# Attention and a cosine-gated FFN on one core: attention matmuls merged into bursts of fixed order, the weight conversion redistributed, softmax sums moved to PSUM

## The chip, the cores and the metric

The kernel runs on one core of a Trainium2 chip. The metric is device time in microseconds (us). Three timed executions gave 1001.33, 1002.23 and 1008.99 us (median 1002.23); a further one was taken by the hardware profiler.

## The reference, cut to what matters

Eight batches, eight heads, 576 positions, head size 64. The first four heads see the last 32 positions, the other four see every 32nd position; softmax, then the FFN with `h * cos(h)`. All in float32.

```python
scores = scale * np.matmul(q, k.transpose(0, 1, 3, 2))
scores = np.where(masks[None], scores, -1e9)
attn = np.exp(scores - np.max(scores, axis=-1, keepdims=True))
attn = attn / (np.sum(attn, axis=-1, keepdims=True) + 1e-09)
x = np.matmul(attn, v) ...          # (8*576, 512) after joining the heads
h = x @ w_in                        # 4608 x 2048
out = (h * np.cos(h)) @ w_out       # 4608 x 512
```

## The kernel before, in words

**FFN.** The 4608 tokens are cut in 12 blocks of 384 (index `j`), the 2048 hidden columns in 16 slices of 128 (index `f`). One pair (j, f) is a chunk. `hidden` makes 12 matmuls into one of two PSUM banks `h` (L345): the float32 operands are split in a high and a low fp32r part, and three products of the parts are summed for four slices of the depth. Then ScalarE rounds h/2pi to an integer (L349), VectorE takes the remainder (L350), ScalarE the sine (L353), VectorE multiplies by `h` (L356) and thereby frees the bank, ScalarE cuts the high part `g_hi` (L359) and GpSimd the low part `g_lo` (L360). `outer` makes 9 matmuls into three accumulators (L367); it runs three chunks (`LAG`) behind `hidden`.

**Attention.** 80 units, ten for each batch: four strided ones (heads with every 32nd position) and six local ones. A unit is a generator of three steps: (1) its score matmuls into a PSUM bank (L238 local, L279 strided) and its softmax; (2) transposes of the probabilities (L246 local, L291 strided) and a copy to SBUF; (3) the products with v (L254 local, L303 strided) and a copy, and a DMA to the tensor `xT` in DRAM, from which `load_x` reads the FFN's blocks. The softmax of the main part is a chain of eleven instructions: mask added (L193, VectorE), maximum (L194, VectorE), subtraction (L195, GpSimd), two Silu (L203, L204, ScalarE), their combination (L205, VectorE), square (L208, ScalarE), sum (L210), 1e-9 added (L211), reciprocal (L212, all VectorE), scaling (L214, GpSimd).

**Stages.** First the 20 units of batches 0 and 1 alone (`plain`: the mask is put in by a matmul, exp is used, and small `keep_busy` matmuls fill TensorE, L417). Then the blocks j = 0 and 1, chunk by chunk in turn, while the weights are brought in: `load_weight` takes 128x512 float64 values as two int32 words and puts them together as float32 (L116, L119 and L125 on VectorE, L124 on ScalarE), cuts the high part (L129, ScalarE) and the low part (L130, GpSimd); 32 of these, in two buffers (`cv`), two for each f. `need_weights` places those of f so that VectorE starts them no earlier than the remainder of chunk (0, f-2). Then the main part: blocks 2 to 11, 160 chunks, the first three still within the loading part; the 60 units of batches 2 to 7 run beside them. Here the score bank is one tile, cleared once (L181) and kept; the transposes have another bank and the products a third.

**Order.** `schedule` gives each unit three places among the chunks: its start from the line through `KNOTS` ((chunk, unit number) pairs), step 2 up to three chunks later, step 3 one chunk after that. This sets the order in which the program names the instructions; the framework that places them may move an instruction of TensorE ahead of others that it expects to wait. Every engine then runs its own list in order, with semaphores between the engines.

Of the kernel before, what the change touches and what calls it, by code (L numbers as in the profile page):

```python
# [12 lines left out]
F32 = mybir.dt.float32  # L13
F32R = mybir.dt.float32r
BF16 = mybir.dt.bfloat16
I32 = mybir.dt.int32
AF = mybir.ActivationFunctionType
ALU = mybir.AluOpType
AX = mybir.AxisListType

B, H, S, D = 8, 8, 576, 64
# [3 lines left out]
P = 128  # L25
# [31 lines left out]

KNOTS = ((LAG, 0), (9.5, 8), (25, 16), (121, 56), (131, 60))
UNIT_LAG = 3
LOAD_AT = 13  # L60
# [8 lines left out]
def attention_cos_ffn(ctx, tc, qkl, vl, qkvs, w_in, w_out, eye, eye16, mask_l0, mask_l, mask_s, out):  # L69
# [41 lines left out]
    def load_weight(cv, src, hi, lo, after):  # L111

        raw = cv.tile([P, 512, 2], I32, name="raw")
        nc.sync.dma_start(out=raw.rearrange("p n w -> p (n w)"), in_=src)
        low, top = raw[:, :, 0], raw[:, :, 1]
        first = nc.vector.tensor_scalar(out=low, in0=low, scalar1=29, scalar2=None, op0=ALU.logical_shift_right)  # L116
        if after is not None:
            order(first, after, "weights no earlier than they are needed")
        nc.vector.scalar_tensor_tensor(  # L119
            out=low, in0=top, scalar=-0x80000000, in1=low, op0=ALU.bitwise_and, op1=ALU.bitwise_or  # L120
        )


        nc.scalar.activation(out=top.bitcast(F32), in_=top.bitcast(F32), func=AF.Copy, scale=2.0 ** -112)  # L124
        nc.vector.scalar_tensor_tensor(  # L125
            out=low, in0=top, scalar=3, in1=low, op0=ALU.logical_shift_left, op1=ALU.bitwise_or
        )
        w = low.bitcast(F32)
        nc.scalar.copy(out=hi, in_=w)  # L129
        nc.gpsimd.tensor_tensor(out=lo, in0=w, in1=hi.bitcast(F32), op=ALU.subtract)  # L130

    weights = 0

    def need_weights(cv, f):
        nonlocal weights
        for f in range(weights, f + 1):
# [6 lines left out]
            weights = f + 1  # L143

    class Attention:

        def __init__(self, stack, plain, scores, transposed, products, ld_bufs):

            self.plain = plain
            self.ld, self.wk = (
                stack.enter_context(tc.tile_pool(name=name, bufs=bufs, side="right", reuse_waits="tile"))
                for name, bufs in (("ld", ld_bufs), ("wk", 2))
            )
            self.scores, self.transposed, self.products = (
                itertools.cycle(kind) for kind in (scores, transposed, products)
            )
            self.turns, self.kept = itertools.cycle(range(len(scores))), {}
            self.pn_s = itertools.cycle(pn_s)  # L160
            self.x_t = {}

        def bank(self, kind):
# [19 lines left out]

        def softmax(self, s, mask, n, w, pn=None):
            t = self.wk.tile([P, SU * GB], F32, name="t_sb")[:, :n * w].rearrange("p (t w) -> p t w", w=w)
# [23 lines left out]
            z = sm.tile([P, SU], F32, name="z")  # L209
            nc.vector.tensor_reduce(out=z[:, :n], in_=e, op=ALU.add, axis=AX.X)  # L210
            nc.vector.tensor_scalar(out=z[:, :n], in0=z[:, :n], scalar1=1e-9, scalar2=None, op0=ALU.add)  # L211
            nc.vector.reciprocal(out=z[:, :n], in_=z[:, :n])  # L212
            pn = e if pn is None else pn
# [11 lines left out]
        def local(self, b, p, u):  # L225
# [8 lines left out]
            for t in range(LU):  # L234
                for j in range(2):
                    rows = slice(64 * j, 64 * j + 64)
                    lo = STRIDE if u + t == 0 else 0
                    self.scored = nc.tensor.matmul(  # L238
                        s_ps[rows, t * KW + lo:(t + 1) * KW], q_t[rows, QB * t:QB * (t + 1)],
                        k_t[rows, QB * t + lo:QB * t + KW], start=not self.plain, stop=True, skip_group_check=True,  # L240
                    )
            pn = self.softmax(s_ps[:, :LU * KW].rearrange("p (t w) -> p t w", w=KW), mask, LU, KW)
            yield
            t_ps = self.bank(self.transposed)
            for t in range(LU):
                nc.tensor.transpose(t_ps[:KW, t * P:(t + 1) * P], pn[:, t], ident)  # L246
            pt = self.wk.tile([P, LU * P], F32, name="pt")
# [4 lines left out]
            for t in range(LU):  # L252
                for j in range(2):
                    nc.tensor.matmul(  # L254
                        a_ps[64 * j:64 * j + 64, t * QB:(t + 1) * QB], v_t[:, t, j],
                        pt[:KW, t * P + 64 * j:t * P + 64 * j + QB], start=True, stop=True, skip_group_check=True,
                    )
            nc.scalar.copy(out=x_t, in_=a_ps[:, :LU * QB])
# [3 lines left out]
        def strided(self, b, p, u):  # L262
# [11 lines left out]
            for t in range(SU):  # L274
                for i in range(2):
                    if SU * u + t // 2 * 2 + i >= NG:
                        continue
                    rows = slice(64 * i, 64 * i + 64)
                    self.scored = nc.tensor.matmul(  # L279
                        s_ps[64 * i:64 * i + GB, t * GB:(t + 1) * GB], q_t[rows, t], k_t[rows, t],  # L280
                        start=not self.plain, stop=True, skip_group_check=True,
                    )
            pn = next(self.pn_s)
            self.softmax(
                s_ps[:, :SU * GB].rearrange("p (t w) -> p t w", w=GB), mask,
                SU, GB, pn[:, :, :GB],
            )
            yield
            t_ps = self.bank(self.transposed)
            for t in range(0, SU, 2):  # L290
                nc.tensor.transpose(t_ps[:, t * GP:(t + 2) * GP], pn[:, t:t + 2].rearrange("p t k -> p (t k)"), ident)  # L291
            pt = self.wk.tile([P, LU * P], F32, name="pt")
# [7 lines left out]
            for t in range(real):  # L300
                for j in range(2):
                    keys = slice(64 * j, 64 * j + GB)
                    nc.tensor.matmul(  # L303
                        a_ps[64 * j:64 * j + 64, t * GB:(t + 1) * GB], v_t[keys, t],
                        pt[keys, t * GB:(t + 1) * GB], start=True, stop=True, skip_group_check=True,
                    )
            x_v = x_t.rearrange("p (a r) -> p a r", r=STRIDE)
# [33 lines left out]
    def hidden(j, f, x_hi, x_lo):  # L341
        h = ps_h.tile([P, 512], F32, name="h")[:, :TB]
        ops = [(w, x, c) for c in range(NKC) for w, x in ((wi_h, x_hi), (wi_h, x_lo), (wi_l, x_hi))]
        for i, (w, x, c) in enumerate(ops):
            nc.tensor.matmul(h, w[:, f, c], x[c], start=(i == 0), stop=(i == len(ops) - 1))  # L345

# [16 lines left out]
    def outer(j, f, g_hi, g_lo, acc):  # L363
        for t in range(NTT):
            ts = slice(t * P, (t + 1) * P)
            for i, (g, w) in enumerate(((g_hi, wo_h), (g_hi, wo_l), (g_lo, wo_h))):
                nc.tensor.matmul(  # L367
                    acc[t], g[:, ts], w[:, f], start=(f == 0 and i == 0), stop=(f == NFC - 1 and i == 2)
                )
            if f == NFC - 1:  # L370
# [16 lines left out]

    def schedule(units, knots, lag):

# [3 lines left out]
        for n, (at, unit) in enumerate(zip(begun, units)):  # L393
            second = min([at + lag] + begun[n + 2:n + 3])
            for stage in (at, second, second + 1):
                steps.setdefault(stage, []).append((n, unit))
        return steps

    def step(steps, n):
        for _, unit in steps.get(n, ()):  # L400
            next(unit, None)

    with ExitStack() as loading:
        cv = loading.enter_context(tc.tile_pool(name="cv", bufs=2))
        with ExitStack() as stack:

            ps = stack.enter_context(tc.tile_pool(name="ps", bufs=1, space=bass.MemoryType.PSUM, reuse_waits="tile"))
            att = Attention(
                stack, True, ((ps_h, "h"), (ps_h, "h"), (ps, "acc0")), ((ps_o, "acc0"), (ps_o, "acc1")),
                ((ps_o, "acc2"), (ps, "acc3")), ld_bufs=3,  # L410
            )
            steps = schedule(att.units(0) + att.units(1), ((0, 0), (20, 20)), 2)
            spare = ps.tile([P, 512], F32, name="acc2")

            def keep_busy(n, after):
                for _ in range(n):
                    mm = nc.tensor.matmul(  # L417
                        spare[:64], warm, warm.unsqueeze(1).broadcast_to([P, 8, 64]), start=True, stop=True
                    )
# [146 lines left out]
```

## Time and profile before

| | |
|---|---|
| timed executions | 1001.33, 1002.23, 1008.99 us |
| the profiled execution | 1007.06 us, of which the span from first to last instruction is 1005.2 us |
| mean granted TensorE clock | 0.992 |
| busy: TensorE, VectorE, ScalarE, GpSimd | 983.1, 472.4, 502.9, 382.3 us |

A row of a group reads: line, engine, operation, written tile <- read tiles, shape, count | busy us, mean ns of one | idle time of the engine before them and what ended it. A row of the timeline reads: start in us, duration in us, engine, line, operation, count, and in brackets the idle time before it and what ended it. Matmuls are pipelined, so the distance from one start to the next, not the duration, is what a matmul costs. A row of windows reads: stretch, its length, then busy us (and instructions) of TensorE, its weight loads, VectorE, ScalarE and GpSimd, the granted clock, the DMA share and GB/s.

### The profile page before, as it was taken

What the parts mean: (1) busy time and instruction counts of PE and PEld (TensorE: products, weight loads), DVE (VectorE), ACT (ScalarE), POOL (GpSimd) and SP (SyncE); (2) the same over time, 40 slices, a digit from 0 to 9 for tenths busy, and PEclk for the clock granted to TensorE, in tenths of its full rate; (3) what the DMA queues carried; (4) which work ended last, traced back from release to release, by engine and by line L of the source; (5) the groups of instructions that cost most, each with busy time, mean ns of one, the idle gap of its engine ahead of it and who ended that gap; (6) DMA issues with size and microseconds to landing.
All of it is one profiled execution on the core that took longest, in us unless ns stands there. A gap on an engine that the chain in (4) does not pass through costs nothing.

```text
span 1005.2 us, 17775 instructions
## 1 busy us (share of the span) xinstructions
PE 983.1 (98%) x6890; PEld 845.1 (84%) x6890; DVE 472.4 (47%) x1005; ACT 502.9 (50%) x1043; POOL 382.3 (38%) x418
## 2 busy tenths in 40 slices
PE   8989999999999999999999999999999999999998
PEld 5778887798888888888888888888888888889997
DVE  5856677645454444434444344434443444422222
ACT  3555555546555545545455454544544545433433
POOL 2555454544443443333333343333333333422222
PEclk9999999999999999999999999999999999999999
DMA  7863333222332222212211222211221221100000
GB/s 244 274 200 111 123 105 105 84 84 77 94 101 96 61 79 89 60 60 69 66 49 51 80 68 64 88 50 53 91 59 39 81 61 47 50 10 1 33 1 31
DMA packets 48228, 80.14 MB, mean 80 GB/s; under 512 B 5904, under 2 KB 33296, under 8 KB 48144
## 3 DMA queue, kind: packets, MB, share of 16 engines
q1 hardware_dynamic: 38208, 69.35, 22.4%
q10 hardware_dynamic: 9936, 9.65, 2.8%
q8 instruction: 54, 0.88, 0.4%
q14 instruction: 30, 0.25, 0.1%
HBM read 60.11 MB, written 18.87 MB: 79 GB/s over the span
## 4 chain that ended last, share of the span: by engine, by line
PE 81%; DMA 2%; DVE 2%; ACT 1%; issue 0%; ACTq 0%; DVEq 0%
PE h L345 36%; PE acc L367 34%; PE acc L238 3%; DMA raw<-in_w_out 2%; PE acc L279 2%; PE acc L254 2%; PE acc L303 2%; PE acc L246 1%; DVE raw L116 1%; PE acc L291 1%; DVE raw L119 0%; DVE r L356 0%; ACT r L353 0%; ACT raw L124 0%; ACT r L349 0%
## 5 line engine op out<-in xcount | busy, mean ns | idle before, releaser
L360 POOL TENSOR_TENSOR g_lo<-r,g_hi 128x384 fp32r<-128x384 f32 x192 | 197.3, 1028 | 442.0 <-issue 295.1
L345 PE MATMUL h<-x_hi,wi_h 128*128 128x384 f32 x768 | 272.3, 355 | 10.7 <-DVE r L356 10.7
L345 PE MATMUL h<-x_lo,wi_h 128*128 128x384 f32 x768 | 261.0, 340 | 0.0
L345 PE MATMUL h<-x_hi,wi_l 128*128 128x384 f32 x768 | 260.5, 339 | 0.0
L350 DVE SCALAR_TENSOR_TENSOR r<-r,h 128x384 f32<-128x384 int32 x192 | 106.0, 552 | 300.3 <-ACT r L349 278.2
L367 PE MATMUL acc<-wo_l,g_hi 128*128 128x512 f32 x576 | 227.0, 394 | 0.0
L367 PE MATMUL acc<-wo_h,g_hi 128*128 128x512 f32 x576 | 224.9, 391 | 0.3 <-ACT g_hi L359 0.3
L367 PE MATMUL acc<-wo_h,g_lo 128*128 128x512 f32 x576 | 224.0, 396 | 0.0
L349 ACT ACTIVATE r<-h 128x384 int32<-128x384 f32 x192 | 93.9, 489 | 188.0 <-PE h L345 173.8
L345 PEld LDWEIGHTS h<-x_hi,wi_h 128*128 128x128 f32 x768 | 145.4, 189 | 25.6 <-DVE r L356 15.9
L353 ACT ACTIVATE r<-r,quarter 128x384 f32<-128x384 f32 x192 | 117.9, 614 | 87.4 <-DVE r L350 87.1
L345 PEld LDWEIGHTS h<-x_lo,wi_h 128*128 128x128 f32 x768 | 145.6, 190 | 3.2
L345 PEld LDWEIGHTS h<-x_hi,wi_l 128*128 128x128 f32 x768 | 145.7, 190 | 0.6
L356 DVE TENSOR_TENSOR r<-r,h 128x384 f32<-128x384 f32 x192 | 106.0, 552 | 74.3 <-ACT r L353 72.6
L359 ACT CAST g_hi<-r 128x384 fp32r<-128x384 f32 x192 | 98.3, 512 | 83.1 <-DVE r L356 82.8
L367 PEld LDWEIGHTS acc<-wo_h,g_lo 128*128 128x128 f32 x576 | 108.0, 188 | 22.3
L367 PEld LDWEIGHTS acc<-wo_h,g_hi 128*128 128x128 f32 x576 | 108.3, 188 | 18.7 <-ACT g_hi L359 0.6
L367 PEld LDWEIGHTS acc<-wo_l,g_hi 128*128 128x128 f32 x576 | 108.0, 188 | 18.1
L336 POOL TENSOR_TENSOR x_lo<-x_raw,x_hi 128x384 fp32r<-128x384 f32 x48 | 50.1, 1048 | 105.2 <-DVE x_hi L335 102.7
L203 ACT ACTIVATE e_sb<-t_sb,shift 128x288 f32<-128x288 f32 (+1 forms) x60 | 32.7, 545 | 48.6 <-POOL t_sb L195 46.4
L335 DVE CAST x_hi<-x_raw 128x384 fp32r<-128x384 f32 x48 | 21.7, 458 | 50.9 <-DMA x_raw<-xT 48.1
L195 POOL TENSOR_TENSOR t_sb<-t_sb,mx 128x288 f32<-128x288 f32 (+1 forms) x60 | 41.5, 692 | 9.2 <-DVE mx L194 8.0
(66 smaller groups left out, 873.1 us busy)
## 6 DMA issues: line engine op xcount, KB each, us to landing
qk<-in_qkvs SPq DMA_DIRECT2D x32, 324.0 KB, 3.1
qk<-in_qkl SPq DMA_DIRECT2D x48, 208.0 KB, 2.6
x_raw<-xT SPq DMA_DIRECT2D x48, 192.0 KB, 2.4
out<-o SPq DMA_DIRECT2D x36, 256.0 KB, 2.1
raw<-in_w_in SPq DMA_DIRECT2D x16, 512.0 KB, 3.7
raw<-in_w_out SPq DMA_DIRECT2D x16, 512.0 KB, 3.7
v<-in_vl SPq DMA_DIRECT2D x48, 144.0 KB, 2.3
xT<-x_t ACTq DMA_DIRECT2D x16, 288.0 KB, 3.2
```

The costliest lines, as they stand in the source:

```text
L195: nc.gpsimd.tensor_tensor(out=t, in0=t, in1=mx[:, :n].unsqueeze(2).broadcast_to([P, n, w]), op=ALU.subtract)
L203: nc.scalar.activation(out=e, in_=t, func=AF.Silu, bias=shift1, scale=0.0625)
L238: self.scored = nc.tensor.matmul(s_ps[rows, t * KW + lo:(t + 1) * KW], q_t[rows, QB * t:QB * (t + 1)], k_t[rows, QB * t + lo:QB * t + KW], ...
L336: nc.gpsimd.tensor_tensor(out=lo, in0=raw, in1=hi.bitcast(F32), op=ALU.subtract)
L345: nc.tensor.matmul(h, w[:, f, c], x[c], start=(i == 0), stop=(i == len(ops) - 1))
L349: nc.scalar.activation(out=k, in_=h, func=AF.Copy, scale=1.0 / (2.0 * math.pi), bias=0.25)
L350: red = nc.vector.scalar_tensor_tensor(out=r, in0=k, scalar=-2.0 * math.pi, in1=h, op0=ALU.mult, op1=ALU.add)
L353: sin = nc.scalar.activation(out=r, in_=r, func=AF.Sin, bias=quarter)
L356: nc.vector.tensor_tensor(out=r, in0=r, in1=h, op=ALU.mult)
L359: nc.scalar.copy(out=g_hi, in_=r)
L360: nc.gpsimd.tensor_tensor(out=g_lo, in0=r, in1=g_hi.bitcast(F32), op=ALU.subtract)
L367: nc.tensor.matmul(acc[t], g[:, ts], w[:, f], start=(f == 0 and i == 0), stop=(f == NFC - 1 and i == 2))
```

## The change

Three things are changed.

*Bursts.* In the main part `schedule` now lists 63 bursts. Burst k holds step 2 of unit k-2, step 3 of unit k-3 and step 1 of unit k. Its chunk comes from new `KNOTS`. `in_turn` fixes the order of TensorE for all matmuls of the main part, blocks 2 to 11 and the attention beside them, as the program names them.

*Weights.* The shift of the low word (L116) becomes an activation on ScalarE; the low part (L130) moves from GpSimd to VectorE. The order behind the remainder of chunk (0, f-2) is now put on the second instruction (L119), not on the first.

*Sums.* L210 and L211 write the softmax sums to PSUM, and L212 reads them there: in the main part in the last six columns of the score bank, in the plain part in eight slots of the bank `spare`, whose `keep_busy` matmuls are cut from 512 to 448 columns.

```diff
-KNOTS = ((LAG, 0), (9.5, 8), (25, 16), (121, 56), (131, 60))
-UNIT_LAG = 3
+KNOTS = ((3, 0), (12, 11), (28, 19), (60, 31), (76, 39), (124, 59), (140, 63))
+UNIT_LAG = 2
...
-        first = nc.vector.tensor_scalar(out=low, in0=low, scalar1=29, scalar2=None, op0=ALU.logical_shift_right)
+
+        nc.scalar.activation(
+            out=low, in_=low.bitcast(U32), func=AF.Copy, scale=2.0 ** -29 * (1.0 - 2.0 ** -16),
+            bias=7.5 * 2.0 ** -16 - 0.5,
+        )
+        first = nc.vector.scalar_tensor_tensor(
+            out=low, in0=top, scalar=-0x80000000, in1=low, op0=ALU.bitwise_and, op1=ALU.bitwise_or
+        )
         if after is not None:
             order(first, after, "weights no earlier than they are needed")
-        nc.vector.scalar_tensor_tensor(
-            out=low, in0=top, scalar=-0x80000000, in1=low, op0=ALU.bitwise_and, op1=ALU.bitwise_or
-        )
...
-        nc.gpsimd.tensor_tensor(out=lo, in0=w, in1=hi.bitcast(F32), op=ALU.subtract)
+        nc.vector.tensor_tensor(out=lo, in0=w, in1=hi.bitcast(F32), op=ALU.subtract)
...
+    turn = None
+
+    def in_turn(mm):
+
+        nonlocal turn
+        if turn is not None:
+            order(mm, turn, "in turn")
+        turn = mm
+        return mm
...
+            self.pe = (lambda mm: mm) if plain else in_turn
...
-            nc.vector.tensor_reduce(out=z[:, :n], in_=e, op=ALU.add, axis=AX.X)
-            nc.vector.tensor_scalar(out=z[:, :n], in0=z[:, :n], scalar1=1e-9, scalar2=None, op0=ALU.add)
-            nc.vector.reciprocal(out=z[:, :n], in_=z[:, :n])
+
+            total = next(self.totals)[:, :n] if self.plain else bank[:, 512 - SU:][:, :n]
+            nc.vector.tensor_reduce(out=total, in_=e, op=ALU.add, axis=AX.X)
+            nc.vector.tensor_scalar(out=total, in0=total, scalar1=1e-9, scalar2=None, op0=ALU.add)
+            nc.vector.reciprocal(out=z[:, :n], in_=total)
...
-                    self.scored = nc.tensor.matmul(
+                    self.scored = self.pe(nc.tensor.matmul(
...
-            nc.tensor.matmul(h, w[:, f, c], x[c], start=(i == 0), stop=(i == len(ops) - 1))
+            mm = nc.tensor.matmul(h, w[:, f, c], x[c], start=(i == 0), stop=(i == len(ops) - 1))
+            if j >= 2:
+                in_turn(mm)
...
+    def schedule(units, begun, lag):
+
+
+        steps = {}
+        for k, at in enumerate(begun):
+            steps.setdefault(at, []).extend(units[m] for m in (k - lag, k - lag - 1, k) if 0 <= m < len(units))
+        return steps
...
+            spare = ps.tile([P, 512], F32, name="acc2")
...
+                totals=[spare[:, 512 - SU * n:][:, :SU] for n in range(1, 9)],
...
-                        spare[:64], warm, warm.unsqueeze(1).broadcast_to([P, 8, 64]), start=True, stop=True
+                        spare[:64, :448], warm, warm.unsqueeze(1).broadcast_to([P, 7, 64]), start=True, stop=True
...
-        steps = schedule([unit for b in range(2, B) for unit in att.units(b)], KNOTS, UNIT_LAG)
+        units = [unit for b in range(2, B) for unit in att.units(b)]
+        begun = np.interp(range(len(units) + UNIT_LAG + 1), [n for _, n in KNOTS], [at for at, _ in KNOTS])
+        steps = schedule(units, begun.astype(int).tolist(), UNIT_LAG)
```

The old `schedule` is kept under the name `in_stages` for the plain part.

More of the change, by code (lines that the diff above doesn't have):

```diff
@@ L16 @@
 I32 = mybir.dt.int32
+U32 = mybir.dt.uint32
 AF = mybir.ActivationFunctionType
@@ L143, in need_weights, with __init__ @@
             weights = f + 1
+    turn = None
[5 more added lines that the diff above has]
+        return mm
     class Attention:
-        def __init__(self, stack, plain, scores, transposed, products, ld_bufs):
+        def __init__(self, stack, plain, scores, transposed, products, ld_bufs, totals=()):
             self.plain = plain
+            self.pe = (lambda mm: mm) if plain else in_turn
             self.ld, self.wk = (
@@ L161, in __init__ @@
             self.x_t = {}
+            self.totals = itertools.cycle(totals)
         def bank(self, kind):
@@ L182, in score_bank, with softmax @@
             return self.kept[n]
-        def softmax(self, s, mask, n, w, pn=None):
+        def softmax(self, bank, mask, n, w, pn=None):
+            s = bank[:, :n * w].rearrange("p (t w) -> p t w", w=w)
             t = self.wk.tile([P, SU * GB], F32, name="t_sb")[:, :n * w].rearrange("p (t w) -> p t w", w=w)
@@ L237, in local @@
                     lo = STRIDE if u + t == 0 else 0
-                    self.scored = nc.tensor.matmul(
+                    self.scored = self.pe(nc.tensor.matmul(
                         s_ps[rows, t * KW + lo:(t + 1) * KW], q_t[rows, QB * t:QB * (t + 1)],
                         k_t[rows, QB * t + lo:QB * t + KW], start=not self.plain, stop=True, skip_group_check=True,
-                    )
-            pn = self.softmax(s_ps[:, :LU * KW].rearrange("p (t w) -> p t w", w=KW), mask, LU, KW)
+                    ))
+            pn = self.softmax(s_ps, mask, LU, KW)
             yield
@@ L245, in local @@
             for t in range(LU):
-                nc.tensor.transpose(t_ps[:KW, t * P:(t + 1) * P], pn[:, t], ident)
+                self.pe(nc.tensor.transpose(t_ps[:KW, t * P:(t + 1) * P], pn[:, t], ident))
             pt = self.wk.tile([P, LU * P], F32, name="pt")
@@ L253, in local @@
                 for j in range(2):
-                    nc.tensor.matmul(
+                    self.pe(nc.tensor.matmul(
                         a_ps[64 * j:64 * j + 64, t * QB:(t + 1) * QB], v_t[:, t, j],
                         pt[:KW, t * P + 64 * j:t * P + 64 * j + QB], start=True, stop=True, skip_group_check=True,
-                    )
+                    ))
             nc.scalar.copy(out=x_t, in_=a_ps[:, :LU * QB])
@@ L278, in strided @@
                     rows = slice(64 * i, 64 * i + 64)
-                    self.scored = nc.tensor.matmul(
+                    self.scored = self.pe(nc.tensor.matmul(
                         s_ps[64 * i:64 * i + GB, t * GB:(t + 1) * GB], q_t[rows, t], k_t[rows, t],
                         start=not self.plain, stop=True, skip_group_check=True,
-                    )
+                    ))
             pn = next(self.pn_s)
[L284 to L287, printed above, removed]
+            self.softmax(s_ps, mask, SU, GB, pn[:, :, :GB])
             yield
@@ L290, in strided @@
             for t in range(0, SU, 2):
-                nc.tensor.transpose(t_ps[:, t * GP:(t + 2) * GP], pn[:, t:t + 2].rearrange("p t k -> p (t k)"), ident)
+                self.pe(nc.tensor.transpose(
+                    t_ps[:, t * GP:(t + 2) * GP], pn[:, t:t + 2].rearrange("p t k -> p (t k)"), ident
+                ))
             pt = self.wk.tile([P, LU * P], F32, name="pt")
@@ L302, in strided @@
                     keys = slice(64 * j, 64 * j + GB)
-                    nc.tensor.matmul(
+                    self.pe(nc.tensor.matmul(
                         a_ps[64 * j:64 * j + 64, t * GB:(t + 1) * GB], v_t[keys, t],
                         pt[keys, t * GB:(t + 1) * GB], start=True, stop=True, skip_group_check=True,
-                    )
+                    ))
             x_v = x_t.rearrange("p (a r) -> p a r", r=STRIDE)
@@ L366, in outer @@
             for i, (g, w) in enumerate(((g_hi, wo_h), (g_hi, wo_l), (g_lo, wo_h))):
-                nc.tensor.matmul(
+                mm = nc.tensor.matmul(
                     acc[t], g[:, ts], w[:, f], start=(f == 0 and i == 0), stop=(f == NFC - 1 and i == 2)
                 )
+                if j >= 2:
+                    in_turn(mm)
             if f == NFC - 1:
@@ L386, in accumulators, with in_stages @@
         return [pool.tile([P, DM], F32, name=f"acc{t}") for t in range(NTT)]
-    def schedule(units, knots, lag):
+    def in_stages(units, knots, lag):
         begun = np.interp(range(len(units)), [n for _, n in knots], [at for at, _ in knots]).astype(int).tolist()
@@ L395, in schedule @@
             for stage in (at, second, second + 1):
-                steps.setdefault(stage, []).append((n, unit))
+                steps.setdefault(stage, []).append(unit)
+        return steps
[3 more added lines that the diff above has]
+            steps.setdefault(at, []).extend(units[m] for m in (k - lag, k - lag - 1, k) if 0 <= m < len(units))
         return steps
     def step(steps, n):
-        for _, unit in steps.get(n, ()):
+        for unit in steps.get(n, ()):
             next(unit, None)
@@ L410, in attention_cos_ffn @@
                 ((ps_o, "acc2"), (ps, "acc3")), ld_bufs=3,
+                totals=[spare[:, 512 - SU * n:][:, :SU] for n in range(1, 9)],
             )
-            steps = schedule(att.units(0) + att.units(1), ((0, 0), (20, 20)), 2)
-            spare = ps.tile([P, 512], F32, name="acc2")
+            steps = in_stages(att.units(0) + att.units(1), ((0, 0), (20, 20)), 2)
             def keep_busy(n, after):
```

## The prediction

> **What bounds the kernel now.** I read the page's shares first, then the chain that ended last, then busy time by stage.
>
> ```profile
> PE 983.1 (98%) x6890; PEld 845.1 (84%) x6890; DVE 472.4 (47%) x1005; ACT 502.9 (50%) x1043; POOL 382.3 (38%) x418
> PE 81%; DMA 2%; DVE 2%; ACT 1%; issue 0%; ACTq 0%; DVEq 0%
> ...
> 52.00:205.00 153.00, 139.42 (x730) 121.76 (x727) 103.39 (x159) 84.68 (x160) 78.64 (x67) 0.97 0.37 119
> 205.00:300.00 95.00, 95.00 (x762) 80.93 (x761) 48.42 (x117) 54.86 (x119) 40.03 (x49) 1.00 0.30 90
> 300.00:865.00 565.00, 565.00 (x4043) 488.79 (x4042) 245.81 (x551) 283.86 (x602) 207.65 (x239) 1.00 0.22 65
> 900.00:950.00 50.00, 50.00 (x252) 45.19 (x251) 13.89 (x25) 20.23 (x39) 12.15 (x12) 1.00 0.05 17
> ```
>
> TensorE sets the end. From 205 to 865 us, where FFN chunks and attention run side by side, it is busy all the time. From 900 to 950 no attention is left: 252 matmuls are 12 chunks of 21, so a chunk costs 50/12 = 4.17 us. That work is fixed. What can change is the attention's share of TensorE, idle time that the new order brings, and the loading stage (52 to 205 us), where TensorE is idle for 13.6 us.
>
> **Merged bursts: what they save.** The timeline of TensorE shows what it costs to leave the FFN's full-width matmuls and to return:
>
> ```profile
> 407.58 0.40 PE L367 MATMUL acc<-wo_l,g_hi 128*128 128x512 f32 x1
> 407.82 0.40 PE L367 MATMUL acc<-wo_h,g_lo 128*128 128x512 f32 x1
> 408.14 0.91 PE L303 MATMUL acc<-pt,v 54*64 54x54 f32 x24
> 408.98 0.44 PE L345 MATMUL h<-x_hi,wi_h 128*128 128x384 f32 x1
> 409.26 0.34 PE L345 MATMUL h<-x_lo,wi_h 128*128 128x384 f32 x1
> 409.44 0.35 PE L345 MATMUL h<-x_hi,wi_l 128*128 128x384 f32 x1
> ...
> 402.72 0.49 PE L291 MATMUL acc<-ident,pn_s 128*128 128x128 f32 x3
> 403.14 0.71 PE L279 MATMUL acc<-qk 64*54 64x54 f32 x18
> ...
> 223.69 0.81 PE L279 MATMUL acc<-qk 64*54 64x54 f32 x24
> ...
> 877.60 0.57 PE L254 MATMUL acc<-pt,v 96*64 96x64 f32 x12
> ```
>
> One `acc` matmul to the next is 0.24; ahead of the products it is 0.32, so entering costs about 0.09 (0.08 by these rounded rows). After the burst the first `h` matmul takes 0.28 where the next takes 0.18: leaving costs about 0.11. The attention stands in 135 separate stretches, from the one at 223.69 to the one at 877.60; 83 open with scores or products and pay the entry, 52 with transposes, which are full-width and don't. In 26 stretches transposes lead over to scores or products, for which I count the same 0.09. Before: 135 x 0.11 + 83 x 0.09 + 26 x 0.09 = 24.6 us. After, 63 bursts stand at 61 different chunks; each opens with transposes, has one such change and one exit: 61 x 0.20 = 12.2. Saved: **12.4 us**. The matmuls themselves stay (the 24 products take 0.84 us from 408.14 to 408.98, either way).
>
> **Merged bursts: what they may cost.** `in_turn` takes away the freedom to put other work ahead of a matmul that waits. Burst k's scores go into the one score bank, and the sums of unit k-1 now lie in the same tile until L212 has read them. Before, the next scores waited for L193 alone; now I take it that they wait for L212. The trace doesn't show such a wait for other columns of a tile, only for the same ones, so both ends stay in the range. How long from the end of the scores to the end of L212:
>
> ```profile
> 246.98 0.66 PE L238 MATMUL acc<-qk 64*64 64x64 f32 x12
> ...
> 247.69 0.46 DVE L193 TENSOR_TENSOR t_sb<-acc,ml 128x288 f32<-128x288 f32 x1 [1.09 <-PE acc L238]
> ...
> 254.67 0.18 DVE L212 RECIPROCAL z<-z 128x3 f32<-128x3 f32 x1
> ...
> 302.54 0.49 DVE L193 TENSOR_TENSOR t_sb<-acc,ms 128x324 f32<-128x324 f32 x1 [1.15 <-PE acc L279]
> ...
> 307.91 0.19 DVE L212 RECIPROCAL z<-z 128x6 f32<-128x6 f32 x1
> ...
> 226.65 1.28 ACT L203 ACT_TABLE_LOAD   x1
> ```
>
> In the dense stretch it is 247.64 to 254.85, 7.2 us; with room it is 302.54 to 308.10, 5.6. I take 6.3, as the FFN's instructions on VectorE and ScalarE thin out when TensorE waits. By `KNOTS`, bursts 0 to 11 start at chunks 3, 3, 4, 5, 6, 7, 7, 8, 9, 10, 11, 12, and later ones are at least two chunks apart. Two chunks are 8.3 us, over 7.2: no wait there. One chunk apart, TensorE does 4.17 + 0.11 + transposes 0.42 (402.72 to 403.14) + products 0.6 (0.57 at 877.60, 0.84 for the longer ones) = 5.3 before the next scores: it waits 1.0 us, nine times, **9** (0.3 to 1.9 each: 3 to 17). Twice two bursts share a chunk. Burst 1 comes straight behind burst 0, whose softmax also loads the table (1.28): 5.6 + 1.28 + 0.1 = **7**. Burst 6 has burst 4's transposes and burst 3's products ahead, 1.1: 6.3 - 1.1 = **5**. A wait of two microseconds or more also leaves TensorE slow:
>
> ```profile
> 106.11 0.40 PE L367 MATMUL acc<-wo_h,g_lo 128*128 128x512 f32 x1
> 108.56 0.51 PE L345 MATMUL h<-x_hi,wi_h 128*128 128x384 f32 x1 [2.06 <-DVE r L356]
> ...
> 112.07 0.40 PE L345 MATMUL h<-x_hi,wi_l 128*128 128x384 f32 x1
> ...
> PE h L345 <- DVE r L356: 10.7, 11, 2.1
> ```
>
> From 108.56 to 112.07 eleven `h` matmuls come 0.32 apart, against 0.18 above: 1.5 us. (The last row, from the list of waits, says how much TensorE waited for the `h` banks in all.) Two such waits: **3**. Sum 24 us (17 to 35). Against 12.4 saved, the main part comes out 11.6 us longer.
>
> On this point the Trainium skill (PSUM — Partial Sum Buffer, PSUM bank collisions raise a hardware error) says that engines are to be kept apart by bank and 32-partition quadrant, not by address. By that rule the wait is there, as in the sum; no run here shows it so far.
>
> **Weights.**
>
> ```profile
> L119 DVE SCALAR_TENSOR_TENSOR raw<-raw 128x512 int32<-128x512 int32 x28 | 24.7, 883 | 0.5
> L116 DVE TENSOR_SCALAR raw<-raw 128x512 int32<-128x512 int32 x28 | 23.6, 845 | 16.1 <-DMA raw<-in_w_out 8.7 <-DMA raw<-in_w_in 7.3
> L125 DVE SCALAR_TENSOR_TENSOR raw<-raw 128x512 int32<-128x512 int32 x28 | 21.9, 785 | 10.2 <-ACT raw L124 9.8
> L130 POOL TENSOR_TENSOR wi_l<-raw,wi_h 128x512 fp32r<-128x512 f32 x14 | 19.0, 1356 | 24.6 <-ACT wi_h L129 24.6
> L124 ACT ACTIVATE raw<-raw 128x512 f32<-128x512 f32 x28 | 18.9, 673 | 26.0 <-DVE raw L119 24.1 <-POOL wi_l L130 1.5
> ...
> L349 ACT ACTIVATE r<-h 128x384 int32<-128x384 f32 x192 | 93.9, 489 | 188.0 <-PE h L345 173.8
> L353 ACT ACTIVATE r<-r,quarter 128x384 f32<-128x384 f32 x192 | 117.9, 614 | 87.4 <-DVE r L350 87.1
> L359 ACT CAST g_hi<-r 128x384 fp32r<-128x384 f32 x192 | 98.3, 512 | 83.1 <-DVE r L356 82.8
> ...
> raw<-in_w_in SPq DMA_DIRECT2D x16, 512.0 KB, 3.7
> ...
> SPq L114 <- POOL wi_l L130: 60.3, 13, 7.0
> ...
> 106.20 1.29 POOL L130 TENSOR_TENSOR wi_l<-raw,wi_h 128x512 fp32r<-128x512 f32 x1 [3.64 <-ACT wi_h L129]
> ...
> 106.49 1.55 DVE L119 SCALAR_TENSOR_TENSOR raw<-raw 128x512 int32<-128x512 int32 x1
> ...
> 103.27 0.69 DVE L119 SCALAR_TENSOR_TENSOR raw<-raw 128x512 int32<-128x512 int32 x1
> ```
>
> The queue of loads waits for L130 to free a buffer (60.3 us in 13 waits). One turn of a buffer is 3.7 + 0.85 + 0.88 + 0.67 + 0.79 + 0.67 (L129, as L124) + 1.33 = 8.9 us and handoffs; two buffers and two weights for each f make one turn per f, while two chunks need 8.33. L119 beside GpSimd takes 1.55, alone 0.69. After: the shift on ScalarE as L124, 0.67; L119 and L125 about 0.75 with GpSimd's half of the work gone; the subtraction, not shown on VectorE, between 0.69 (L119 alone) and 1.36 (GpSimd), taken as 0.74. Turn: 3.7 + 0.67 + 0.75 + 0.67 + 0.75 + 0.67 + 0.74 = 7.95, 0.9 less, times 14 = 13, about what TensorE idles. But ScalarE's work for two chunks and two weights rises to 2 x (0.49 + 0.61 + 0.51) + 6 x 0.67 = 7.2 of 8.33, and its queue, with L349 and L353 in it, now stands behind a first instruction that waits for the DMA. I take half: **-6** (-13 to +2).
>
> Against the move, the Trainium skill (SBUF — State Buffer, Who interferes with whom) says that a VectorE instruction with two SBUF inputs contends with a GpSimd instruction that reads SBUF. The row at 106.49 agrees. By that rule the moved subtraction keeps colliding with `g_lo`: perhaps -3 instead of -6, an estimate.
>
> **Sums.**
>
> ```profile
> L211 DVE TENSOR_SCALAR z<-z x80: 141/170/1025, 9.7 to 864.1; 128x3 f32<-128x3 f32 x48, 128x6 f32<-128x6 f32 x32
> ```
>
> L211 takes 0.17 as a median and up to 1.03. In PSUM the long ones may go. In the main part that is off TensorE's path except through the wait above. In the plain part it eases VectorE, but the sums share a bank with `keep_busy`, so each may wait for the other: **0** (-3 to +4).
>
> **Sum.** -12.4 + 24 - 6 + 0 = +5.6. The profiled execution took 1007.06 (span 1005.2 and 1.9 around it): 1012.7. It lies 4.8 above the median of the runs, 1002.23, which makes 1007.9: **1008 us**.
>
> **Rivals.** *Faster, 0.24.* The next scores wait only for L193 (other columns of the tile count as free). Then transposes wait instead: unit 0's, one chunk behind its scores, need 5.6 + 1.28 + about 1.0 for the scaling L214 (two of L193's 0.49) = 7.9 after those scores; until then TensorE has a wait for L193 of 0.6, burst 1's scores of 0.7 and a chunk of 4.3: it waits 2.3, and 1.5 for the clock; unit 4's about 1. Main part -12.4 + 4.8; with -6: 993.5, or 989. For it: the program's sums and scores touch no common column. Against: the code treats the bank as one tile. *Slower, 0.32.* ScalarE bounds the loading stage. The 16.1 us that VectorE waits for the DMA at L116 pass to ScalarE, 1.15 for each f; 7.2 + 1.15 = 8.35 is just where the two chunks' 8.33 no longer cover it, and from there one activation for each f (0.67) comes onto the path of the `h` banks: 14 x 0.67 = +9 instead of -6, so 1023. For it: ScalarE already waits 24.1 us at L124 for VectorE. Against: the buffer's turn gets shorter, so the DMA starts earlier. *Forecast, 0.44.*
>
> **Range and chances.** One per cent, 10 us, is about what a measurement of this kernel tells from no change. The forecast spans 994 (17 us of waits, -13 for the weights) to 1019 (35 and -6). The range reaches to 988, the middle of the first rival, and to 1026, a little beyond the second, and so leaves out about 0.1 on either side. Faster by over 1% (under 992): most of the first rival and little else, 0.20. Slower (over 1012): most of the second rival and the upper quarter of the forecast, 0.38. Within: 0.42.
>
> **What would show it.** Right: near 220 to 290 us rows `PE acc L238` or `L279` waiting for `DVE z L212`, the longest 5 to 7 us; 61 stretches of attention; PE idle after 205 of some 20 us; from 52 us less than 13.6 idle before the main part. Wrong: no such waits (the first rival), or `PE h L345 <- DVE r L356` above its present 10.7 us (the second). The forecast also fails if the softmax in the dense stretch is much shorter than 5.6 us or if a later stretch, now without freedom of order, waits as well.

## The result, and the profile after

The changed kernel is slower: 1036.99 us median (1033.39 to 1038.23) against 1005.02 for the kernel before in the same comparison, a ratio of 1.0329 (95% interval 1.0299 to 1.0358). The forecast was 1008, the range 988 to 1026. The profiled execution took 1038.23 us, its span is 1036.4. The kernel before was timed again in each comparison that is told below, with medians from 1002.15 to 1003.52; times from different comparisons are therefore comparable to within 2 or 3 us only.

From the page of the kernel after (busy time, chain by engine), and the windows of its trace:

```profile
PE 984.7 (95%) x6890; PEld 857.9 (83%) x6890; DVE 463.3 (45%) x1005; ACT 520.1 (50%) x1077; POOL 342.5 (33%) x386
PE 75%; DMA 10%; DVE 6%; ACT 6%; issue 1%; POOL 1%; SPq 0%; ACTq 0%; POOLq 0%; DVEq 0%
...
52.00:205.00 153.00, 134.42 (x780) 112.17 (x780) 96.06 (x171) 96.88 (x186) 40.68 (x41) 0.94 0.39 125
205.00:300.00 95.00, 81.44 (x589) 71.34 (x588) 43.47 (x98) 48.31 (x100) 33.89 (x39) 0.89 0.22 68
300.00:865.00 565.00, 559.70 (x4116) 497.21 (x4115) 244.69 (x565) 283.47 (x613) 211.90 (x243) 1.00 0.23 69
```

TensorE's share of the chain fell from 81% to 75%. From 205 to 865 us it now idles for 13.6 + 5.3 = 18.9 us, where it had not idled at all. But fixed windows mix stages when a late start shifts all that follows; a mark that every chunk carries is better. Each chunk has one cut of `g_hi` on ScalarE; here are those of chunks 0, 31, 52 and 191 in order of time, first from the timeline of the kernel before, then of the kernel after.

```profile
68.41 0.52 ACT L359 CAST g_hi<-r 128x384 fp32r<-128x384 f32 x1
...
211.07 0.51 ACT L359 CAST g_hi<-r 128x384 fp32r<-128x384 f32 x1 [0.62 <-DVE r L356]
...
321.99 0.51 ACT L359 CAST g_hi<-r 128x384 fp32r<-128x384 f32 x1 [0.62 <-DVE r L356]
...
997.02 0.51 ACT L359 CAST g_hi<-r 128x384 fp32r<-128x384 f32 x1 [0.62 <-DVE r L356]
```

```profile
90.68 0.51 ACT L380 CAST g_hi<-r 128x384 fp32r<-128x384 f32 x1
...
227.99 0.51 ACT L380 CAST g_hi<-r 128x384 fp32r<-128x384 f32 x1 [0.78 <-DVE r L377]
...
366.37 0.51 ACT L380 CAST g_hi<-r 128x384 fp32r<-128x384 f32 x1 [0.29 <-DVE r L377]
...
1026.97 0.51 ACT L380 CAST g_hi<-r 128x384 fp32r<-128x384 f32 x1 [0.62 <-DVE r L377]
```

The differences give the stages; the other columns are worked out in the same way from the traces of three experiments told below (all in us).

| from chunk to chunk | before | after | plain_sums_sbuf | all_sums_sbuf | single_bursts |
|---|---|---|---|---|---|
| start to 0 (plain attention) | 68.4 | 90.7 | 70.0 | 63.5 | 63.8 |
| 0 to 31 (loading) | 142.7 | 137.3 | 134.5 | 134.4 | 135.9 |
| 31 to 52 (dense bursts) | 110.9 | 138.4 | 138.0 | 120.9 | 109.9 |
| 52 to 191 (the rest) | 675.0 | 660.6 | 660.7 | 660.7 | 662.2 |

After against before: +22.3, -5.4, +27.5, -14.4, together +30.0. The dense bursts lose and the rest gains about as forecast. What the forecast had at nothing, the plain part, is the largest net loss.

Each column is one execution, and the stages do not repeat equally well. The rest takes 660.6 or 660.7 in all nine traces that have the bursts at the places of the changed kernel, and 675.0 in all three that have the places of the kernel before. The plain part is less steady: `plain_sums_sbuf` and `all_sums_sbuf` have the same code there, and chunk 0 comes at 70.0 and at 63.5. The profiled execution of `plain_sums_sbuf` took 1014.4 us, the longest of its ten, whose median is 1007.12. A difference of up to 6.5 us at chunk 0 between two traces is therefore no evidence by itself; the 22.3 are.

In the plain part, the first matmuls of TensorE are, before and after:

```profile
5.83 1.05 PE L279 MATMUL h<-qk 64*54 64x54 f32 x24
6.81 1.48 PE L417 MATMUL acc<-warm 128*64 128x512 bf16 x6
8.22 0.31 PE L173 MATMUL h<-ms,ident 128*128 128x324 bf16 x1
8.46 0.80 PE L279 MATMUL h<-qk 64*54 64x54 f32 x20
```

```profile
5.30 0.86 PE L299 MATMUL h<-qk 64*54 64x54 f32 x24
6.09 0.31 PE L190 MATMUL h<-ms,ident 128*128 128x324 bf16 x1
6.34 0.80 PE L299 MATMUL h<-qk 64*54 64x54 f32 x20
...
13.41 1.33 PE L449 MATMUL acc<-warm 128*64 128x448 bf16 x3
```

Before, six `keep_busy` matmuls stand right behind unit 0's scores, from 6.81 to 8.22. After, the first behind those scores comes at 13.41, though the program names it in the same place: the scores of units 1 to 4 now stand ahead of it. The sums of unit 0 now lie in the bank that these matmuls write. With the plain part's sums out of it, and nothing else changed (`plain_sums_sbuf` below), the six are back behind unit 0's scores, at 5.91. So the operand has changed the order in which the framework lists TensorE's work, and not only the waits between the engines. From 0 to 50 us, before and then after:

```profile
0.00:50.00 50.00, 45.98 (x636) 30.43 (x636) 36.91 (x111) 23.52 (x56) 20.48 (x30) 0.97 0.82 259
```

```profile
0.00:50.00 50.00, 40.10 (x510) 26.15 (x510) 29.86 (x80) 22.32 (x48) 10.09 (x18) 0.86 0.76 235
```

126 matmuls fewer are done by 50 us, and the granted clock is 0.86 instead of 0.97. The lists of waits for the first 85 us, before and then after, show the direct part of it, in both directions, and what it does to the softmax:

```profile
POOL pn_s L214 <- DVE z L212: 14.2, 3, 9.1
...
POOL e_sb L214 <- DVE z L212: 4.6, 5, 1.9
```

```profile
POOL pn_s L234 <- DVE z L232: 20.0, 5, 8.9
POOL e_sb L234 <- DVE z L232: 14.2, 9, 2.9
...
DVE acc L230 <- PE acc L449: 4.0, 5, 1.7
PE acc L449 <- DVE z L232: 1.7, 3, 0.8
```

The sums wait 4.0 us for `keep_busy` and `keep_busy` 1.7 us for the sums: 5.7 us of direct waits, for 22 us lost. GpSimd, whose scaling is the last step of the softmax, waits 34.2 us for the reciprocals where it had waited 18.8 (18.9 in `plain_sums_sbuf`): the results of the softmax come later.

### The profile page after: what moved, and what is told of

The parts are those of the page before. It is cut to its first block, busy times and chain, and to the rows that moved or that the text cites. A ratio compares the mean times of both kernels' runs of the same rounds, so it can differ in the third digit from the quotient of the medians.

```text
span 1036.4 us, 17747 instructions
## 1 busy us (share of the span) xinstructions
PE 984.7 (95%) x6890; PEld 857.9 (83%) x6890; DVE 463.3 (45%) x1005; ACT 520.1 (50%) x1077; POOL 342.5 (33%) x386
## 4 chain that ended last, share of the span: by engine, by line
PE 75%; DMA 10%; DVE 6%; ACT 6%; issue 1%; POOL 1%; SPq 0%; ACTq 0%; POOLq 0%; DVEq 0%
PE h L364 33%; PE acc L388 32%; DMA raw<-in_w_out 5%; DMA x_raw<-xT 2%; PE acc L322 2%; DMA raw<-in_w_in 2%; PE acc L299 2%; PE acc L258 2%; PE acc L274 2%; DVE wi_l L135 1%; PE acc L266 1%; ACT raw L129 1%; ACT raw L118 1%; DVE r L371 1%; ACT r L374 1%
## 5 line engine op out<-in xcount | busy, mean ns | idle before, releaser
L388 PE MATMUL acc<-wo_h,g_lo 128*128 128x512 f32 x576 | 227.4, 396 | 1.3 <-POOL g_lo L381 1.3
```

The costliest lines, as they stand in the source:

```text
L388: mm = nc.tensor.matmul(acc[t], g[:, ts], w[:, f], start=(f == 0 and i == 0), stop=(f == NFC - 1 and i == 2))
```

## The experiments

Two theories were set up for the plain part. **Theory 1**: the sums in the bank of `keep_busy` cost it. **Theory 2**: the new weight conversion does, since its instructions stand in ScalarE's and VectorE's queues beside the plain softmax. For the dense bursts the question was whether the sums in the score bank make the scores wait.

**Sums of the plain part back in SBUF** (`plain_sums_sbuf`).

```diff
-            total = next(self.totals)[:, :n] if self.plain else bank[:, 512 - SU:][:, :n]
+            total = z[:, :n] if self.plain else bank[:, 512 - SU:][:, :n]
```

> The changed kernel with the sums of the plain part (batches 0 and 1) back in SBUF; the main part's sums stay in PSUM. Theory 1 (the plain part lost its 22 us because the sums and the keep-busy matmuls share a bank and wait for each other): 1015 us, with the first chunk about 22 us earlier. Theory 2 (it lost them because the first weights' subtraction and shift now stand in the queues of VectorE and ScalarE beside the plain softmax): 1035 to 1037, the first chunk no earlier.

Measured: 1007.12 us, 1.0052 (1.0028 to 1.0076). This one operand is worth 29.9 us by the medians; chunk 0 comes at 70.0 instead of 90.7, in an execution 7.3 us above its median. Theory 1 holds: the operand does it. What the weights have to do with it is asked below.

**Sums of the main part back in SBUF** (`main_sums_sbuf`).

```diff
-            total = next(self.totals)[:, :n] if self.plain else bank[:, 512 - SU:][:, :n]
+            total = next(self.totals)[:, :n] if self.plain else z[:, :n]
```

> The changed kernel with the main part's sums back in SBUF; the plain part's sums stay in PSUM. If the 26 us lost in the dense stretch are the next scores' wait for L232 in the score bank, that wait is gone, transposes wait some 5 us in its place, and the time is about 1037 - 20 = 1017 us. Rival (the dense stretch is lost to the fixed order as such, the softmax being too long for the places given): waits for the softmax move to the transposes in full, 1030 to 1037.

Measured: 1020.45 us, 1.0157 (1.0112 to 1.0202), 16.5 less than after. No scores wait for L232 any more, and chunks 31 to 52 take 121.3 us instead of 138.4.

**All sums in SBUF** (`all_sums_sbuf`): both edits, `total = z[:, :n]`.

> The changed kernel with all softmax sums back in SBUF: bursts, fixed order and the new weight conversion alone. Theory 1: both gains add, 1037 - 22 - 20 = 995 us, faster than before by 1%. Theory 2: 1017 us.

Measured: 991.05 us, 0.9881 (0.9852 to 0.991). Against `plain_sums_sbuf` the main part's sums are worth 16.1 us, as above, so the two prices add up. TensorE's longest waits for the attention are now those of the transposes:

```profile
PE acc L266 <- POOL e_sb L234: 3.3, 1, 3.3
PE acc L308 <- POOL pn_s L234: 2.4, 1, 2.4
```

**The old weight conversion in the changed kernel** (`weights_old`): the shift back on VectorE, the subtraction back on GpSimd, the order back on the shift.

```diff
-        nc.scalar.activation(
-            out=low, in_=low.bitcast(U32), func=AF.Copy, scale=2.0 ** -29 * (1.0 - 2.0 ** -16),
...
+        first = nc.vector.tensor_scalar(out=low, in0=low, scalar1=29, scalar2=None, op0=ALU.logical_shift_right)
...
-        nc.vector.tensor_tensor(out=lo, in0=w, in1=hi.bitcast(F32), op=ALU.subtract)
+        nc.gpsimd.tensor_tensor(out=lo, in0=w, in1=hi.bitcast(F32), op=ALU.subtract)
```

> The changed kernel with the weight conversion of before (shift on VectorE, subtraction on GpSimd). Theory 1: the loading stage loses its gain of about 5 us and the plain part stays as slow, 1042 us. Theory 2: the plain part is back at its old pace, 1037 - 22 + 5 = 1020 us.

Measured: 1031.72 us, 1.0282 (1.0256 to 1.0307), 5.3 less than after, where theory 1 had 1042 and theory 2 had 1020: neither is right alone. Chunk 0 comes at 84.1, against 90.7 and, in `main_sums_sbuf` with the same plain part as after, 93.0. Beside sums in the bank of `keep_busy`, the new conversion thus makes the plain part longer, by 6.6 in the first pair, and gains 4.6 of it back in loading (141.9 us from chunk 0 to 31, against 137.3). With the sums in SBUF it does not: chunk 0 comes at 63.5 to 70.0 with the new conversion (five traces) and at 66.0 and 68.4 with the old one. So theory 2 has a part in the loss, but only on top of theory 1. The other 3 us of this pair lie in the dense bursts (135.2 from chunk 31 to 52, against 138.4); five traces with the same main part spread there from 134.8 to 138.4, so they need no cause in the weights.

**The new weight conversion alone, on the kernel before** (`weights_alone`): the same diff the other way round.

> The kernel before with the new weight conversion alone. By the buffer's shorter turn: the loading stage (chunk 0 to chunk 31) 5 us shorter, 998 to 999 us. Rival (ScalarE bounds the stage): 1005 us or more.

Measured: 996.79 us, 0.995 (0.9931 to 0.9969), a little under the 998 to 999 that the shorter turn was to give. From the groups by line of its trace, 55 to 205 us, and its waits:

```profile
L117 ACT ACTIVATE raw<-raw 128x512 int32<-128x512 uint32 x26 | 17.5, 672 | 21.6 <-DMA raw<-in_w_in 17.4 <-DMA raw<-in_w_out 4.0
L134 DVE TENSOR_TENSOR wo_l<-raw,wo_h 128x512 fp32r<-128x512 f32 x14 | 10.7, 767 | 4.2 <-ACT wo_h L133 4.0
L134 DVE TENSOR_TENSOR wi_l<-raw,wi_h 128x512 fp32r<-128x512 f32 x14 | 9.6, 682 | 0.0
...
PE h L349 <- DVE r L360: 4.3, 8, 0.9
```

The shift takes 0.67 us, the subtraction 0.68 and 0.77 as means, and TensorE waits 4.3 us for the `h` banks instead of 10.7. ScalarE does wait 21.4 us for the DMA, as the slower rival said, but that does not reach TensorE.

**The merged bursts alone** (`bursts_alone`): sums in SBUF and the old weight conversion, both as above.

> The changed kernel with the sums in SBUF and the weight conversion of before: the bursts and the fixed order alone. If 12.4 us are saved by fewer changes and some 5 us lost to waits of the first transposes: 1002 - 7 = 995 us. If the all-in-SBUF kernel's gain came from the weights and from the plain part: 1002 us.

Measured: 997.16 us, 0.9928 (0.9905 to 0.9951): a gain of 5.6 us over the 1002.80 of its comparison, less than the 7 that were expected. Its dense bursts take 120.4 us and its rest 660.6, as in `all_sums_sbuf`.

**The plain sums alone, on the kernel before** (`plain_sums_alone`): they are written to the bank of `keep_busy`, the rest is as before.

```diff
-            nc.vector.tensor_reduce(out=z[:, :n], in_=e, op=ALU.add, axis=AX.X)
...
+            total = next(self.totals)[:, :n] if self.plain else z[:, :n]
+            nc.vector.tensor_reduce(out=total, in_=e, op=ALU.add, axis=AX.X)
...
-                        spare[:64], warm, warm.unsqueeze(1).broadcast_to([P, 8, 64]), start=True, stop=True
+                        spare[:64, :448], warm, warm.unsqueeze(1).broadcast_to([P, 7, 64]), start=True, stop=True
```

> The kernel before with one part of the change alone: the plain part's sums in the bank of the keep-busy matmuls, those cut to 448 columns. Theory 1a: it loses what the changed kernel lost there, 1004 + 20 to 30 = 1024 to 1034 us. Theory 2 (the new weight conversion is needed for the loss): 1004 to 1010 us.

Measured: 1022.44 us, 1.0216 (1.0178 to 1.0253), so this part by itself makes the kernel slower, with neither bursts nor weights changed. By itself it costs 20.3 us, though (the kernel before took 1002.15 in this comparison), the low end of the 20 to 30 that were expected and a third less than the 29.9: with the old conversion chunk 0 comes at 83.3 here and at 84.1 in `weights_old`, with the new one at 90.7 and 93.0. Its window from 0 to 50 us:

```profile
0.00:50.00 50.00, 37.04 (x539) 24.24 (x539) 29.61 (x86) 19.26 (x44) 15.88 (x23) 1.00 0.78 249
```

The granted clock is 1.00, and still TensorE has done 539 matmuls instead of 636. Up to here the loss is not the clock. Later the clock adds to it: in the same trace it is 0.66 from 50 to 60 us and 0.54 from 70 to 83.

**The plain sums in another bank of PSUM** (`plain_own_bank`): in the unit's own score bank, as in the main part.

```diff
-            total = next(self.totals)[:, :n] if self.plain else bank[:, 512 - SU:][:, :n]
+            total = bank[:, 512 - SU:][:, :n] if self.plain else bank[:, 512 - SU:][:, :n]
```

> The changed kernel with the plain part's sums still in PSUM, but in the last columns of each unit's own score bank in place of the bank of the keep-busy matmuls. Theory 1a (the loss comes from sharing the keep-busy bank): the plain part is as fast as with sums in SBUF, 1007 to 1010 us. Theory 1b (sums in PSUM cost it wherever they lie, since a score bank or any bank is held until the reciprocal): 1025 to 1037 us.

Measured: 1012.02 us, 1.0112 (1.0078 to 1.0146). 25.0 of the 29.9 us are saved though the sums stay in PSUM. So most of the price is for sharing the bank with `keep_busy`, not for PSUM. The plain part has three score banks in turn, so the next scores do not wait for this unit's sums. About 5 us remain. TensorE's list of waits has three of the mask matmuls (L190) for L232, 1.8 us together; what the rest is, no run says.

**No `keep_busy` behind the first ten** (`no_keep_busy`), in the changed kernel, and **the same with all sums in SBUF** (`sbuf_no_keep_busy`).

```diff
-BUSY = (10, 6, 5, 3, 2, 2, 2) + 8 * (1,)
+BUSY = (10,) + 14 * (0,)
```

> The changed kernel without the 28 keep-busy matmuls behind the scores (the first ten stay); sums in PSUM as changed. Theory 1a: with nothing left to share the bank, most of the 22 to 30 us come back, less what TensorE loses by running slow in the plain part: 1010 to 1020 us. Theory 1b: 1035 us or more.

> All sums in SBUF, without the 28 keep-busy matmuls behind the scores. It prices what those matmuls are worth by themselves. If the changed kernel without them (1025) is slow only for want of them, they are worth 1025 - 1007 = 18 us, and this one comes to 991 + 18 = 1009 us. If they are worth little, 991 to 995 us, and the sums in their bank cost more than the shared bank explains.

Measured: 1025.44 us, 1.0243 (1.0221 to 1.0264), and 1009.05 us, 1.0052 (1.0031 to 1.0073). The second is what was expected; the first lies between the two expectations. Their windows from 0 to 50 us, without and with the sums in SBUF, and that of `all_sums_sbuf`, which has both SBUF and `keep_busy`:

```profile
0.00:50.00 50.00, 37.67 (x438) 27.32 (x439) 27.90 (x78) 22.04 (x49) 12.04 (x20) 0.68 0.70 218
```

```profile
0.00:50.00 50.00, 36.42 (x452) 25.66 (x452) 29.49 (x81) 22.77 (x51) 13.03 (x21) 0.81 0.73 232
```

```profile
0.00:50.00 50.00, 45.14 (x676) 31.67 (x677) 36.56 (x114) 26.51 (x63) 18.43 (x28) 1.00 0.85 271
```

With sums in SBUF these small matmuls are worth 1009.05 - 991.05 = 18.0 us. With sums in their bank they do harm: leaving them out gains 1036.99 - 1025.44 = 11.6. Together 29.6, nearly the 29.9: by this account 18 us of use are lost and 12 are harm. It is an account of medians. At chunk 0 the traces show the use (63.5 with and 80.7 without), but of the harm only 4.2 (90.7 and 86.5). Without `keep_busy` the bank of the plain sums hardly matters by the medians: 1025.44 - 1009.05 = 16.4 is the price of the main part's sums alone. Chunk 0 of these two traces lies 5.8 us apart (86.5 and 80.7), less than the 6.5 by which the same plain part differed above.

**One burst for each chunk, all sums in SBUF** (`single_bursts`), to take away the shared chunks behind which the remaining waits stood.

```diff
-KNOTS = ((3, 0), (12, 11), (28, 19), (60, 31), (76, 39), (124, 59), (140, 63))
+KNOTS = ((3, 0), (13, 10), (15, 11), (28, 19), (60, 31), (76, 39), (124, 59), (140, 63))
...
-            total = next(self.totals)[:, :n] if self.plain else bank[:, 512 - SU:][:, :n]
+            total = z[:, :n]
```

> All sums in SBUF, and the first bursts placed one for each chunk (chunks 3, 4, 5 to 13, then 15, 16, 18), so that no two share a chunk. If the two shared chunks cost the waits of 3.3 and 2.4 us for the transposes and the slow clock behind them: 991 - 6 = 985 us, under both kernels. If those units are only pushed on and the next blocks of x come late: 991 us or more.

Measured: 983.72 us, 0.9792 (0.9753 to 0.9832), the best of all and better than both kernels. Its windows show TensorE all but without gaps, and its list of waits has no transposes left that wait for GpSimd:

```profile
205.00:300.00 95.00, 94.92 (x858) 82.91 (x858) 50.87 (x124) 57.69 (x126) 39.56 (x48) 1.00 0.31 92
300.00:865.00 565.00, 565.00 (x4026) 502.28 (x4023) 243.35 (x548) 282.29 (x605) 211.92 (x240) 1.00 0.22 65
```

**The same knots with the main part's sums in PSUM** (`single_bursts_main_psum`; the edit is against `single_bursts`).

```diff
-            total = z[:, :n]
+            total = z[:, :n] if self.plain else bank[:, 512 - SU:][:, :n]
```

> The same places of the bursts, plain sums in SBUF, main sums in PSUM as changed. By the prediction's sum the two shared chunks cost 7 + 5 and 3 for the clock, the other nine 1.0 each: 1007 - 13 = 994 us, with waits of the scores for L232 of 10 to 13 us left. If the wait were the same wherever the bursts stand: 1005 us or more.

Measured: 1007.38 us, 1.004 (1.0011 to 1.0069), not the 994 that was expected and no better than `plain_sums_sbuf` with its 1007.12. The list of waits says why:

```profile
PE acc L258 <- DVE z L232: 9.0, 7, 3.0
PE acc L299 <- DVE z L232: 6.7, 4, 3.0
```

The wait of 6.8 behind burst 0 is gone, but there are eleven waits now, 15.7 us together, where the kernel after has nine with 17.5. These knots put thirteen bursts one chunk behind the last instead of nine, and one chunk is too short for the softmax each time.

## Why the prediction was wrong, point by point

**The sums in the plain part: the step that failed.** The prediction said: "the sums share a bank with `keep_busy`, so each may wait for the other: **0** (-3 to +4)". They cost 29.9 us in the changed kernel and 20.3 alone. The wait itself was seen, but only its direct part was priced; that is 5.7 us, near the +4. Two consequences were left out. `keep_busy` is there to fill the gaps in which TensorE waits for data, and it can only do so when it is free to go; tied to the sums it comes late (13.41 instead of 6.81). And what stands behind a `keep_busy` matmul in TensorE's list waits with it: in the kernel after one waits 0.70 us for L232, to 35.31, and the next unit's mask follows at 35.78, and through it that unit's scores and sums. The prediction should have asked what those matmuls are worth (18.0 us) before tying them to the softmax. The rule by banks from the Trainium skill that the prediction weighed for the score bank (PSUM — Partial Sum Buffer, PSUM bank collisions raise a hardware error) applies to this bank as well: its two writers share no column, and the rows show them waiting in both directions. Whether the chip demands it or only the program, which keeps the bank as one tile, no run here shows. I had not carried the rule over. How much of the 29.9 us is the lower clock, how much the changed order of the list and how much waiting is not separated: in the first 50 us the clock was 0.86 in the kernel after, but 1.00 in `plain_sums_alone`, which still lost.

The signs that the prediction named for being right came, but for one: a longest wait of the scores of 6.8 us, 61 stretches of attention in the trace, 18.9 us of idle TensorE after 205, and no more than 10.7 us of waiting for the `h` banks (9.3). The one that did not come, less than 13.6 us of idle TensorE from 52 us to the main part, is mixed with the plain part by the late start (18.6 from 52 to 205). All of them look at the main part or at the loading; none looked at the part whose term was 0.

**The rest of the sum held.** With that step at nothing the forecast was 1008; `plain_sums_sbuf`, which is the change without that step, takes 1007.12. That the two agree to 1 us is in part luck, since the terms were off in both directions. One by one:

*Waits of the dense bursts, +24.* The main part as a whole came out 27.5 - 14.4 = 13.1 us longer, against 24 - 12.4 = 11.6. The waits are where they were forecast. From the timeline of the kernel after, the scores of bursts 0, 1, 6, 10 and 11, with some of their neighbours, and from its list of waits the two kinds of scores:

```profile
237.87 0.81 PE L299 MATMUL acc<-qk 64*54 64x54 f32 x24
245.43 1.36 PE L299 MATMUL acc<-qk 64*54 64x54 f32 x20 [6.76 <-DVE z L232]
...
247.21 0.52 PE L364 MATMUL h<-x_lo,wi_h 128*128 128x384 f32 x1
247.53 0.52 PE L364 MATMUL h<-x_hi,wi_l 128*128 128x384 f32 x1
...
275.35 0.88 PE L266 MATMUL acc<-ident,e_sb 128*96 128x128 f32 x3 [0.85 <-POOL e_sb L234]
...
280.40 1.23 PE L258 MATMUL acc<-qk 64*64 64x96 f32 x12 [2.92 <-DVE z L232]
...
310.26 0.81 PE L299 MATMUL acc<-qk 64*54 64x54 f32 x24 [2.74 <-DVE z L232]
...
318.49 0.80 PE L299 MATMUL acc<-qk 64*54 64x54 f32 x20 [2.21 <-DVE z L232]
...
PE acc L299 <- DVE z L232: 11.9, 4, 6.8
PE acc L258 <- DVE z L232: 5.6, 5, 2.9
```

Burst 1 waits 6.8 (forecast 7), and the matmuls behind it then run 0.32 apart instead of 0.18, as forecast. Burst 6, the other one in a shared chunk, waits 2.9 for L232 (forecast 5; the transposes ahead of it had waited 0.9 already, at 275.35). The nine bursts one chunk behind the last wait 17.5 - 6.8 - 2.9 = 7.8 together (forecast 9). But they are not alike: two do not wait, five wait 0.2 to 1.2, and bursts 10 and 11 wait 2.74 and 2.21, more than the 1.9 that was given as the most. From burst 12 on no scores wait for L232, as forecast. That a wait of two microseconds or more leaves TensorE slow is right only in part: behind 2.92 and 2.21 the `h` matmuls run 0.32 apart as well, behind the 2.74 at 310.26 they run 0.18 apart. So there are three slow stretches where two were counted.

The experiments put the price of these waits at 16.1 to 16.5 us and not at 24: they come to 17.5 where 9 + 7 + 5 = 21 were forecast, and without them other waits appear, the transposes' 3.3 and 2.4 of `all_sums_sbuf`, which the faster rival had named (2.3 and about 1). That rival gave 989 for scores that do not wait; the kernel in which they do not, `all_sums_sbuf`, takes 991.05.

*Merging, -12.4.* Right, once no wait covers it: `single_bursts` has the new weights and the bursts without the waits, and lies 996.79 - 983.72 = 13.1 us below `weights_alone`. In `all_sums_sbuf`, where transposes wait, 996.79 - 991.05 = 5.7 of it is left. The runs do not separate the merging from the fixed order and the new places of the bursts, which came with it; the rows do show the exits that are saved. A merged burst in the kernel after reads

```profile
409.87 0.39 PE L388 MATMUL acc<-wo_h,g_lo 128*128 128x512 f32 x1
410.10 0.49 PE L266 MATMUL acc<-ident,e_sb 128*96 128x128 f32 x3
410.51 0.57 PE L274 MATMUL acc<-pt,v 96*64 96x64 f32 x12
411.01 0.81 PE L299 MATMUL acc<-qk 64*54 64x54 f32 x24
411.75 0.44 PE L364 MATMUL h<-x_hi,wi_h 128*128 128x384 f32 x1
412.03 0.34 PE L364 MATMUL h<-x_lo,wi_h 128*128 128x384 f32 x1
```

The transposes follow the last `acc` matmul at 0.23, without a pause, and one exit (0.28 to the second `h` matmul, 0.10 more than the usual 0.18) serves all three steps.

*Weights, -6.* `weights_alone` gains 5.0 us by its ratio of 0.995 (3.1 to 6.9 by the interval). Loading takes 140.6 to 142.7 us in the four traces with the old conversion and 133.3 to 137.3 in the ten with the new one. The subtraction on VectorE, taken as 0.74, measured 0.68 and 0.77 in `weights_alone` and 1.05 and 0.74 in the kernel after. The collisions that the rule of the Trainium skill on who interferes with whom (SBUF — State Buffer) foresees are there: in the kernel after a subtraction that starts at 129.87 takes 1.29 beside a `g_lo` of GpSimd from 129.33 to 130.61, where others take 0.68. But the -3 that was estimated by this rule was too little. The slower rival's time was nearest to the result, but its mechanism was not there: TensorE's wait for the `h` banks fell to 9.3 us in the kernel after, where that rival wanted more than 10.7.

*L231 in PSUM.* The long executions of the small addition are gone, as supposed, and no run shows a gain by it: in `all_sums_sbuf`, with L231 in SBUF, the longest is 0.98 again, and that kernel is faster than both. Its answer by source line in the kernel after:

```profile
L231 DVE TENSOR_SCALAR acc<-acc x80: 154/169/173, 9.5 to 878.1; 128x3 f32<-128x3 f32 x48, 128x6 f32<-128x6 f32 x32
```

## What to carry to other kernels

Before a result is moved into a bank that another engine writes, ask what that engine then waits for, and what stands behind it in its list: the price is not the wait between the two, but everything that is queued behind it, and the use of work that was meant to fill gaps. A step whose interval is given as "each may wait for the other" has no small upper end until the other's worth is known; price the filler by leaving it out. And price a schedule by its closest pair: bursts one chunk apart (about 5.3 us here) cannot share a bank with a softmax of 5.6 to 7.2 without a wait.

## What the runs showed of the hardware that was not expected

Twenty-eight filler matmuls of about 0.24 us each (six from 6.81 to 8.22 in the kernel before) are worth 18.0 us of 1009, and the granted clock of the first 50 us is 1.00 with them and 0.81 without. The same matmuls turn into a loss of 11.6 us when VectorE's sums lie in columns of their bank that they do not touch.
